# A table of corrections to the priorities of a list planner, in a one-core attention and two-layer MoE kernel

## The chip, the cores and the metric

The kernel runs on one core of one Trainium2 chip. The metric is the device time of one execution in microseconds, as the median of the runs shown. The profile comes from one profiled execution, and its times count from the first instruction of the program.

## The reference, cut to what matters

Three stages follow one another; each takes the output of the one before. B, H, S, D are 2, 8, 768, 64, so there are 1536 tokens of 512 numbers, and the hidden width of the two layers is 2048.

```python
# 1: attention: a window of +-16 positions, and 24 block summaries (max of k, mean of v over 32 positions)
k_sum = k.reshape(B, H, nb, block, D).max(axis=3)
v_sum = v.reshape(B, H, nb, block, D).mean(axis=3)
scores = concat(where(|i - j| < 16, q @ k.T / 8, -1e9), q @ k_sum.T / 8 + log(32))
x = softmax(scores) @ concat(v, v_sum)
# 2: first layer: a rational function between two products
h = x @ w_in
g = (a0 + a1*h + a2*h**2 + a3*h**3) / (1 + |b0|*|h| + |b1|*h**2 + 1e-6)
x = g @ w_out
# 3: second layer
h = x @ w_in2
out = (h * clip(h + 3, 0, 6) / 6) @ w_out2
```

The weights arrive as 64-bit floats; the kernel makes 32-bit pairs of them itself.

## The kernel before, in words

**Tiling.** Attention works on 12 groups of 128 tokens (six of each batch). A group has `scores` (TensorE, L407, and the maximum on VectorE, L420), `softmax` (ScalarE L434, GpSimd L438 and L440, VectorE L439), `turn` (TensorE transposes L450, copied out in L454 or L456) and `values` (TensorE L468, split into a high and a low part in L478 and L479). Four groups make one chunk `x` of 512 tokens; there are three chunks c. The block means of v come from TensorE (L347, L374).

**The layers.** `steps` has 96 steps n = (ph, c, i): four phases ph (two halves of the hidden width for each layer), three chunks, eight hidden tiles i of 128. A step has a `first_product` (12 matmuls of 128x512, L513), an activation (`act1` for the first layer, `act2` for the second) and a `second_product` (12 matmuls, L535) that comes three steps, later two pairs of steps, behind. Each value is held as a high and a low part, so each product is three matmuls. Steps 0 to 15 are done one at a time into the PSUM tiles `hs0` and `hs1`; from step 16 on they go in pairs into two double tiles `hb`. After the eighth tile of a chunk the four accumulators `y` are copied out (`evac`, L549 to L570).

**The weights.** `weight(ph, i)` brings one hidden tile in two halves k: one DMA of 512 KB into one of four buffers `raw` (L246), a clamp (L252, VectorE, in phases 1 and 2 GpSimd), a scaling (L254, ScalarE), a shift and an or on the integer words (L256 and L258, VectorE), the high part (L261, ScalarE) and the low part (L263, GpSimd).

**The order.** Nothing is issued while the code above runs: each piece of work is put in a list with `add`, with its engine, a cost in us, what it reads and writes, and whether it takes the port that VectorE and GpSimd share (`port=True`). `order` then makes one list for all engines. `tail[i]` is the sum of the costs on the longest path from operation i to the end. A list scheduler goes forward in planned time; whenever an engine is free, it takes among the operations of that engine that are ready by then (within 0.15 us) the one with the largest `tail`. It leaves no engine idle when something is ready for it. The products are tied to one another by `chain=True` and so keep their order on TensorE; only attention can slip between them. The DMAs go to one queue (SP) in the same manner. On the chip each engine then executes its own share of the list strictly in that order, and waits by semaphores.

**Fill.** Where the plan has TensorE wait over 0.6 us ahead of an operation that has a `fill`, or as long as no chunk x exists, L703 puts matmuls on zeros (128x256, bf16) in front of it, as many as fit the planned wait and at least four.

Of the kernel before, what the change touches and what calls it, by code (L numbers as in the profile page):

```python
# [18 lines left out]
B, H, S, D = 2, 8, 768, 64  # L19
# [3 lines left out]
P = 128  # L23
# [19 lines left out]
PE, DVE, ACT, POOL, SP = "PE", "DVE", "ACT", "POOL", "SP"  # L43
WIRE = 280.0
HOP = 0.1


class Plan:
# [31 lines left out]
    def order(self):  # L80
        ops = self.ops
        n = len(ops)
        after = [[] for _ in range(n)]
        for i, o in enumerate(ops):
            for d in o[3]:
                after[d].append(i)

        def late(d, i):
            return ops[d][5] + (0.0 if ops[d][0] == ops[i][0] else HOP)

        tail = [0.0] * n
        for i in range(n - 1, -1, -1):
            tail[i] = ops[i][1] + max((late(i, j) + tail[j] for j in after[i]), default=0.0)
        missing = [len(o[3]) for o in ops]
        ready = [0.0] * n
        avail = {e: [] for e in (PE, DVE, ACT, POOL, SP)}
        for i in range(n):
            if not missing[i]:
                avail[ops[i][0]].append(i)
        free = dict.fromkeys(avail, 0.0)  # L100
        port = wire = 0.0
        lanes = [0.0] * 8
        dmas = 0
        start = [0.0] * n
        for _ in range(n):
            best = None
            for e, a in avail.items():
                if not a:
                    continue
                when = {i: max(ready[i], port) if ops[i][4] else ready[i] for i in a}  # L110
                t0 = max(free[e], min(when.values()))
                i = max((i for i in a if when[i] <= t0 + 0.15), key=lambda i: (tail[i], -i))
                t = max(t0, when[i])
                if e == SP:
                    t = max(t, lanes[dmas % 8])
                if best is None or t < best[0]:
                    best = (t, e, i)
            t, e, i = best
            us, land = ops[i][1], ops[i][5]
            avail[e].remove(i)  # L120
            start[i] = t
            free[e] = end = t + us
            if ops[i][4]:
                port = end
            if e == SP:
                wire = max(wire, end) + land
                end = wire + 2.2
                lanes[dmas % 8] = end
                dmas += 1
            for j in after[i]:  # L130
                ready[j] = max(ready[j], end + (0.0 if ops[j][0] == e and e != SP else HOP))
                missing[j] -= 1
                if not missing[j]:
                    avail[ops[j][0]].append(j)
        self.start = start
        return sorted(range(n), key=lambda i: (start[i], i))
# [638 lines left out]
```

## Time and profile before

| | us |
|---|---|
| median of 3 runs | 630.49 |
| lowest and highest run | 629.33 and 635.31 |
| span of the profiled execution | 629.6 |
| TensorE matmul busy | 608.4 (97%) |
| VectorE busy | 399.5 (63%) |
| GpSimd busy | 356.1 (57%) |
| ScalarE busy | 347.9 (55%) |

The profile keeps the span alone as the time of its own execution; it stands 0.9 us under the median and 0.3 us over the lowest run, so that sums over the trace can be set against the median directly. Matmuls are pipelined, and the busy time of TensorE counts the fill matmuls too, so 97% isn't a measure of useful work. Shares over the whole span mix stages with different limits.

### The profile page before, as it was taken

The page shows a single profiled execution, that of the slowest core. Times are in us where ns is not written, and L with a number is a line of the kernel's source. Part 1 is how long each engine was busy: PE and PEld are TensorE (multiplying, and loading weights), DVE is VectorE, ACT ScalarE, POOL GpSimd, SP SyncE. Part 2 cuts the span into 40 slices and gives each one's busy share as a digit, 9 for nine tenths or more (in the row PEclk, how much of TensorE's full clock was granted, in tenths as well). Part 3 has the DMA queues.
Part 4 walks back from the last instruction along what each step waited for, and adds up shares of the span by engine and source line. Part 5 has one row for each costly group of instructions (what it writes and reads, how often), then busy time and mean ns, then how long its engine had stood idle before and what let it go on. Part 6 is the DMA issues. An engine that isn't in the chain of part 4 may idle for free.

```text
span 629.6 us, 9837 instructions
## 1 busy us (share of the span) xinstructions
PE 608.4 (97%) x3848; PEld 495.4 (79%) x3848; DVE 399.5 (63%) x622; ACT 347.9 (55%) x604; POOL 356.1 (57%) x277
## 2 busy tenths in 40 slices
PE   9898998999999999999899999999999999999997
PEld 6577776777788887888688888888888888888886
DVE  4689799977648999999699985841364611201211
ACT  2779778885759669676669665431453322211220
POOL 0846978875576886779469887531545422131311
PEclk9899999999999999999899999999999999999999
DMA  9993453220142312321030332400122100000101
GB/s 314 318 290 99 157 170 99 85 84 0 32 134 68 101 53 81 101 67 34 0 101 1 134 93 92 148 3 1 67 68 100 35 0 1 33 35 1 67 1 67
DMA packets 18072, 52.49 MB, mean 83 GB/s; under 512 B 2281, under 2 KB 2761, under 8 KB 18025
## 3 DMA queue, kind: packets, MB, share of 16 engines
q1 hardware_dynamic: 18024, 51.85, 25.7%
q8 instruction: 30, 0.49, 0.3%
q14 instruction: 18, 0.14, 0.1%
HBM read 48.06 MB, written 3.15 MB: 81 GB/s over the span
## 4 chain that ended last, share of the span: by engine, by line
PE 65%; DVE 19%; ACT 7%; issue 4%; POOL 2%; DMA 2%; SPq 0%; DVEq 0%; POOLq 0%; ACTq 0%
PE y L535 29%; PE hb L513 25%; PE hs L513 5%; DVE raw L258 5%; DVE raw L256 4%; DVE t L608 2%; DVE t L600 2%; DMA raw<-in_w 2%; DVE hb L610 1%; PE hs L407 1%; DVE t L601 1%; PE hs L703 1%; PE hs L468 1%; ACT hb L603 1%; ACT hb L605 1%
## 5 line engine op out<-in xcount | busy, mean ns | idle before, releaser
L513 PE MATMUL hb<-xx,wt 128*128 128x512 f32 x960 | 226.5, 392 | 4.0 <-DVE t L612 3.8
L513 PEld LDWEIGHTS hb<-xx,wt 128*128 128x128 f32 x960 | 180.9, 189 | 43.8 <-DVE t L612 5.4
L535 PE MATMUL y<-g,wt 128*128 128x512 f32 x576 | 138.8, 392 | 1.6 <-ACT part L551 1.5
L628 POOL TENSOR_TENSOR g<-t,g 128x1024 fp32r<-128x1024 f32 x24 | 58.2, 2425 | 135.7 <-ACT g L627 126.8
L535 PE MATMUL y<-wt,g 128*128 128x512 f32 x576 | 134.1, 389 | 0.0
L535 PEld LDWEIGHTS y<-g,wt 128*128 128x128 f32 x576 | 107.0, 188 | 24.4 <-ACT part L551 2.2
L535 PEld LDWEIGHTS y<-wt,g 128*128 128x128 f32 x576 | 108.1, 188 | 22.5
L263 POOL TENSOR_TENSOR wt<-raw,wt 128x512 fp32r<-128x512 f32 x62 | 87.1, 1416 | 41.5 <-ACT wt L261 36.7
L625 DVE SCALAR_TENSOR_TENSOR t<-t,hb 128x1024 f32<-128x1024 f32 x24 | 29.3, 1220 | 119.2 <-ACT t L624 119.2
L258 DVE SCALAR_TENSOR_TENSOR raw<-raw 128x512 int32<-128x512 int32 x62 | 76.3, 1241 | 6.9 <-ACT raw L254 5.1
L597 POOL TENSOR_TENSOR q<-q,u 128x512 f32<-128x512 f32 (+1 forms) x32 | 59.9, 1870 | 30.3 <-ACT u L591 29.1
L615 POOL TENSOR_TENSOR g<-t,g 128x512 fp32r<-128x512 f32 (+1 forms) x32 | 62.1, 1941 | 7.6 <-ACT g L614 5.0
L261 ACT ACTIVATE wt<-raw 128x512 fp32r<-128x512 f32 x62 | 41.1, 673 | 44.1 <-DVE raw L258 38.6
L256 DVE TENSOR_SCALAR raw<-raw 128x512 int32<-128x512 int32 x62 | 58.1, 945 | 10.5 <-DMA raw<-in_w 5.3
L624 ACT ACTIVATE t<-hb,lnb 128x1024 f32<-128x1024 f32 x24 | 26.8, 1116 | 66.5 <-PE hb L513 66.5
L627 ACT ACTIVATE g<-t 128x1024 fp32r<-128x1024 f32 x24 | 25.5, 1061 | 57.0 <-PE y L535 56.7
L254 ACT ACTIVATE raw<-raw 128x512 f32<-128x512 f32 x62 | 40.5, 674 | 17.4 <-DVE raw L252 14.0
L513 PE MATMUL hs<-xx,wt 128*128 128x512 f32 x192 | 47.4, 396 | 0.0
L513 PEld LDWEIGHTS hs<-xx,wt 128*128 128x128 f32 x192 | 35.4, 188 | 8.1 <-issue 0.4
L252 DVE TENSOR_SCALAR raw<-raw 128x512 f32<-128x512 f32 x30 | 26.8, 894 | 21.2 <-DMA raw<-in_w 21.2
L434 ACT ACTIVATE s<-s,stat 128x120 f32<-128x120 f32 x72 | 27.3, 382 | 11.3 <-DVE stat L420 11.3
L614 ACT ACTIVATE g<-t 128x512 fp32r<-128x512 f32 (+1 forms) x32 | 27.1, 846 | 7.8 <-DVE t L612 7.6
(111 smaller groups left out, 694.8 us busy)
## 6 DMA issues: line engine op xcount, KB each, us to landing
raw<-in_w SPq DMA_DIRECT2D x62, 512.0 KB, 5.3
out<-part SPq DMA_DIRECT2D x12, 256.0 KB, 2.8
vv<-in_vw SPq DMA_DIRECT2D x6, 384.0 KB
k<-in_kT SPq DMA_DIRECT2D x4, 384.0 KB
tok<-in_vt SPq DMA_DIRECT2D x3, 512.0 KB
q<-in_qT SPq DMA_DIRECT2D x6, 256.0 KB, 7.2
e<-in_kT SPq DMA_DIRECT2D x4, 384.0 KB, 7.9
raw<-in_vt SPq DMA_DIRECT2D x3, 512.0 KB, 6.2
```

Of the source, the lines that this page charges most:

```text
L254: add(ACT, 0.62, lambda hif=hif: nc.scalar.activation(hif, hif, AF.Prelu, scale=REBIAS, alpha=2.0 ** 32), [kr], [(kr, 1)])
L256: add(DVE, 0.38, lambda lo=lo: nc.vector.tensor_single_scalar(lo, lo, 29, op=ALU.logical_shift_right), [kr], [(kr, 0)], port=True)
L258: add(DVE, 0.65, lambda lo=lo, hi=hi: nc.vector.scalar_tensor_tensor(out=lo, in0=hi, scalar=3, in1=lo, op0=ALU.logical_shift_left, op1=ALU ...
L261: add(ACT, 0.62, lambda lof=lof, ph=ph, i=i, cols=cols: nc.scalar.activation(w_of(ph, i)[:, 0, cols], lof, AF.Copy), [kr, (kr, 0)], first)
L263: add(POOL, 1.27, lambda lof=lof, ph=ph, i=i, cols=cols: nc.gpsimd.tensor_tensor(out=w_of(ph, i)[:, 1, cols], in0=lof, in1=w_of(ph, i)[:, ...
L434: nc.scalar.activation(s[:, a, :], s[:, a, :], AF.Exp, scale=-1.0, bias=sm[:, 0, j, a, :], accum_out=sm[:, 1, j, a, :])
L513: mm(ps, lt, rt, start=(k == 0), stop=(k == 11))
L535: mm(y, lt, rt, start=(i == 0 and j == 0), stop=(i == HALF - 1 and j == 2))
L597: add(POOL, us_of(1.27, 2.36), lambda: nc.gpsimd.tensor_tensor(out=q, in0=q, in1=uu, op=ALU.mult), uk, qk, port=True)
L615: add(POOL, us_of(1.27, 2.38), lambda: nc.gpsimd.tensor_tensor(out=gl, in0=t, in1=gh, op=ALU.subtract), tk, gk, port=True)
L625: add(DVE, 1.18, lambda: nc.vector.scalar_tensor_tensor(out=t, in0=t, scalar=6.0, in1=pair_of(a), op0=ALU.min, op1=ALU.mult), hk, tk)
L628: add(POOL, 2.38, lambda: nc.gpsimd.tensor_tensor(out=gl, in0=t, in1=gh, op=ALU.subtract), tk, gk, port=True)
```

## The change: a correction to each priority

The table `LEAD` is a text of 1827 characters, one for each operation in the order in which they are added. A character's code less 80 is a number of microseconds, from -45 (`#`) to 45 (`}`); the mean is -3.9. It is added to `tail`, and the choice among ready operations goes by the sum.

```diff
+LEAD = (
+    '}+IaTnry1ysyL|y|}|S|<|}yxluDegd=GasOM%G1W*sKRKU*kN07&)6+.,C}d&V&&&#vc*Z:[wgQp1:+##%#92=#F#,H#?8A'
...
+    'cbl'
+)
...
         tail = [0.0] * n
         for i in range(n - 1, -1, -1):
             tail[i] = ops[i][1] + max((late(i, j) + tail[j] for j in after[i]), default=0.0)
+        rank = [tail[i] + ord(LEAD[i]) - 80 for i in range(n)]
...
-                i = max((i for i in a if when[i] <= t0 + 0.15), key=lambda i: (tail[i], -i))
+                i = max((i for i in a if when[i] <= t0 + 0.15), key=lambda i: (rank[i], -i))
```

The costs, what depends on what, the buffers and the rule that no engine is left idle stay. The number of fill matmuls follows the planned waits, so it can change with the order.

Some places of the table, decoded: the loads of the keys of the first batch have +44, those of the second -41, -41, -37 and -45. The load of the first half of weight tile 0 has +42, of its second half -3, of the first half of tile 2 -16; the loads of v of groups 0 to 5 have -9, -31, 7, -38, 35 and -5; the load of q of group 4 has 5 (and those of groups 2 and 3 have 2 and -5). The operations of `act1` of steps 0 to 8 have -33 on average, those of `act1` from step 16 on 0.5; the weight operations of phase 2 have 14. The operations of attention groups 0 to 6 have between -12 and -21 on average, of groups 7, 8 and 9 they have 9 to 10.

## Rows read from the trace of the kernel before

**Rows 1.** The page: busy time, share and instructions, and TensorE's slices.

```profile
PE 608.4 (97%) x3848; PEld 495.4 (79%) x3848; DVE 399.5 (63%) x622; ACT 347.9 (55%) x604; POOL 356.1 (57%) x277
PE   9898998999999999999899999999999999999997
```

**Rows 2.** The chain that ended last, in order of time: start, length, what.

```profile
308.45 7.37 PE hb L513 x24
315.82 5.44 PE y L535 x24
...
609.58 16.33 PE y L535 x72
```

**Rows 3.** Windows of L513: stretch, length, PE busy (count), clock, DMA share, GB/s.

```profile
0.00:308.40 308.40, 115.26 (x480) 0.99 0.38 117
```

**Rows 4.** The same windows of L535.

```profile
0.00:308.40 308.40, 105.22 (x432) 0.99 0.38 117
```

**Rows 5.** The same windows of L407, of L468 and of L450.

```profile
0.00:308.40 308.40, 16.23 (x768) 0.99 0.38 117
...
0.00:308.40 308.40, 14.14 (x384) 0.99 0.38 117
...
0.00:308.40 308.40, 13.75 (x96) 0.99 0.38 117
```

**Rows 6.** The same windows of L703, the fill matmuls.

```profile
0.00:50.00 50.00, 11.53 (x84) 0.97 1.00 304
50.00:200.00 150.00, 15.12 (x122) 1.00 0.29 89
200.00:308.40 108.40, 0.00 (x0) 1.00 0.21 68
```

**Rows 7.** Windows of all engines: PE, PEld, DVE, ACT, POOL busy (counts), clock, DMA.

```profile
20.00:40.00 20.00, 16.53 (x269) 13.31 (x267) 13.86 (x53) 13.64 (x47) 14.54 (x17) 0.91 1.04 323
40.00:300.00 260.00, 249.34 (x1891) 202.41 (x1892) 223.82 (x382) 198.05 (x374) 194.88 (x161) 1.00 0.29 91
200.00:250.00 50.00, 48.52 (x213) 39.52 (x212) 46.15 (x39) 38.91 (x44) 36.60 (x24) 1.00 0.26 85
250.00:300.00 50.00, 50.00 (x221) 41.00 (x220) 48.44 (x41) 34.72 (x41) 41.28 (x25) 1.00 0.20 64
```

**Rows 8.** The page's DMA issues: KB of each, us to landing.

```profile
raw<-in_w SPq DMA_DIRECT2D x62, 512.0 KB, 5.3
...
vv<-in_vw SPq DMA_DIRECT2D x6, 384.0 KB
```

**Rows 9.** The chain that ended last, early: values, then the first products.

```profile
33.81 1.15 PE hs L468 x32
...
41.34 5.66 PE hs L513 x24
...
63.03 2.96 PE hs L513 x12
```

**Rows 10.** VectorE's instructions of L256 and L258, each line by itself: duration min/median/max.

```profile
L256 DVE TENSOR_SCALAR raw<-raw x62: 394/732/2635, 27.1 to 495.3; 128x512 int32<-128x512 int32 x62
...
L258 DVE SCALAR_TENSOR_TENSOR raw<-raw x62: 664/696/2936, 33.8 to 497.0; 128x512 int32<-128x512 int32 x62
```

**Rows 11.** Groups of VectorE in 40 to 300: busy, mean ns, idle before.

```profile
L258 DVE SCALAR_TENSOR_TENSOR raw<-raw 128x512 int32<-128x512 int32 x33 | 42.9, 1310 | 1.1
L256 DVE TENSOR_SCALAR raw<-raw 128x512 int32<-128x512 int32 x35 | 31.4, 905 | 6.4 <-POOL wt L263 5.1 <-DMA raw<-in_w 1.2
```

**Rows 12.** The timeline from 294.74: start, length, engine, what, idle before.

```profile
294.74 5.16 DVE L256 TENSOR_SCALAR raw<-raw 128x512 int32<-128x512 int32 x2
...
307.17 1.22 DVE L612 SCALAR_TENSOR_TENSOR t<-hb,t 128x1024 f32<-128x1024 f32 x1
...
308.45 2.07 PE L513 MATMUL hb<-xx,wt 128*128 128x512 f32 x6 [2.32 <-DVE t L612]
```

**Rows 13.** TensorE in a window of 2 us: busy, clock, DMA.

```profile
310.00:312.00 2.00, 2.00 (x6) 0.50 0.00 0
```

More of the change, by code (lines that the diff above doesn't have):

```diff
@@ L45 @@
 HOP = 0.1
+LEAD = (
+    '}+IaTnry1ysyL|y|}|S|<|}yxluDegd=GasOM%G1W*sKRKU*kN07&)6+.,C}d&V&&&#vc*Z:[wgQp1:+##%#92=#F#,H#?8A'
+    "-#K:s}#B'&t6E,0g#S9o.]%/Ei%)zy28L?0ME6&M#K*+*%%#30.#a&#Z@+]&&#+/>]MOJSL)#zMV5UI#>z##KRze$[>(?:#("
+    ",(]c}24(('%'%+<#%'#uQ*G}=1-*-#q9,46%.0q0(i[S;;*&fZyIey=?;L@y9C-a'RHACy]kXn+lv+'FuXuK074?&#6#>1o6"
+    ',#)9##$\\#llhoh#$P/*#d#>%+|#_+O2C`vIta@fr7N:lC^AE>GsW/(>N4`zoCQ}}]}}b}o;vzhX;K<sa}LP^|}M}8vtvt8Me'
+    '+FcMR*#].5O\\$%BRC).)=)#??#8)8T#d:)/E#;#.#*O#9VbJ<<0Ju$##I&#-#C####55%#B##?#.#&CP#a#?))##`#DL>###'
+    "######*%#C##6r$##$D#;*D##*#$)#7,-##*###09&I#4$tH{-32$\\#2,),5##,07#ma'D<%$I;*=##,I:#E##`.H>##}YDs"
+    "JA'//\\7ma++JVY`6.K={JN4x\\@$}f8}}}8A=egtS6s}Hdef}2}?Z61BW$4eFm2X{v#%ag?iz7I#o+6Dq%Y@cUOOT`dSooVm,"
+    "JK#LZnX/RM,+92L######(##&18lM5#5#^X_V_<p]dX}zv}n}exr_(Q3QD#.#)Z6F''7/0)$)),3)B=x`*f6i`d;=#M#&1M>"
+    "&:<P279TSq^8^QFBD,%'#QZnfN'3O,^CGF)^TB7#g#%\\f.#G#b1npsDrvrh#cgsTw;vWd]W#d(AG\\0#WWs5B5>|ut_*9jH{V"
+    'FE89bd^nBXX}{Q(<+Ff17>#-L\\+K=44E}o8B#*[4wT%e*Zj\\,#-+6<wGODOR7}Q?>}+T3(0H@0C+H/0-+8/?E-#;#:G33#)#'
+    "25A-#$#'EED##2-G?IM:<U<4*:h}B^|cv,=<g6#>\\IM>O4-a,||,]zz{-f`r}}}_/qpgq-@}-<{D<t-<@>:mte1qtBtK=E%+"
+    '{p=k[aUz_EXvv^_Rvv,MC0xwfDp[}q}ttcvvw}vjvY]m`C|e|o7[(w\\riNtrmtRACSTp1I%*N0+13wT#AjXV:DyyyyexZ3Hr'
+    'WZ#5L-;,*&K#>O=jci7.h\\>6HASgY7ca_yxiD`ZcNg4Pk/%(&KLjc|^/nAE@|GbusEytFNu#Z2gexTB%%*>)L)eDmoxtcR0t'
+    "xEvygWifde7\\'ceO|}1{ppx{K}gZx8mwXaW]xe}3}im}juyh}x>az1vNx}`{tFhxxMvgG06Bc9ov71gmXYnn(EMFoay3cjKF"
+    '?mpJnHLyycstmhkQ;B^gjjugf}jjkkRcmkkOiKU#YeucfnnOg5q#DEnU\\bD8gWR:J#,#9D#@<}l_m}xZT<s#FyEwqy[XgT}_'
+    '`3e}B\\<{}YY]I,./4?JNLQ_[UpR:k3J420_U}m-=u-HZS-H-`W0-249--:--P#G+(#.3#<5a&<D&<BO)Vq&X.t&{K&x^<kbp'
+    "Kq&E_l]GuDd'ST'E.z,xy,8'H6TKBB-NFxn2CN6_WK4ql}yTqUy}}hfK}}}npDJjX]MpHVkokkdZZ72bkY*%-2=[4P);%p=K"
+    '3+:.^pl2BqROczM7>Bzf3<.eR*:*3I}/RSZ8^A;-8VtJJJJJDeGU@+A=FAku>kd>j>>+@cZ48V2#.0yF+uAD1DFTbOQg5aM8'
+    '}d=46#(#;#?WC/LPh#}mp=vRrVVM#orjwPD}1iiR+\\WKfMh]{}{{[tn}kvqQ}g.uuPz{zvz{uY}czy|zZ=uub&^#etbqpopo'
+    'cbl'
+)
 class Plan:
```

## The prediction

> **What bounds the kernel now.** I read the page's busy shares first, then the chain that ended last, then windows of single lines of TensorE. The page shows TensorE 97% busy and no slice under eight tenths [rows 1], which would leave nothing to an order; but it counts the fill matmuls and the overlap of pipelined matmuls. The chain says where the order matters. From 315.82 to 609.58 it is an unbroken run of pieces of 24 product matmuls, 5.44 us each (293.76 us are 54 of them), and after that 72 more and one eviction [rows 2]. There TensorE never waits; no order can shorten it. One product matmul costs 5.44/24 = 0.2267 us. All that a new order can win lies before 308.4.
>
> What TensorE does in those 308.4 us: 480 + 432 = 912 product matmuls [rows 3, 4], 206.7 us. Scores, values and transposes have 16.2 + 14.1 + 13.8 = 44.1 us [rows 5], a little too much since ends overlap. The fill has 11.5 + 15.1 = 26.7 us [rows 6]. That makes 277.5, and 31 us remain for the clock's warm-up, the block means and bare waits. The fill is the part that the plan itself knows of: L703 issues as many matmuls as fit a wait that the list has. Of it, 11.5 us lie in the first 50 us, where the DMA engines are full (share 1.00 there, 1.04 and 323 GB/s in 20 to 40 [rows 6, 7]), and 15.1 us in 50 to 200, where their share is 0.29 and loads can't be the cause. After 200 there is none.
>
> VectorE is the next in line: 223.8 us busy in 40 to 300, 46.15 and 48.44 us in the last two stretches of 50 [rows 7].
>
> **The change part by part.**
>
> *The table itself.* It is read while the program is built. It adds no instruction, and the list still leaves no engine idle that has something ready. So its direct cost is nothing, and its whole effect is which of several ready operations goes first on an in-order engine, and how many fill matmuls are issued. The number of choices is large at first and small later: before 200, attention, weights and single steps compete on every engine, while in phases 2 and 3 `act2` and a few weights do, with TensorE covering both.
>
> *The DMA queue.* The loads of the second batch's keys go back by about 40, the first half of weight tile 0 forward by 42. The loads without anything to wait for are simply sorted by `tail` plus correction; worked out from the costs in the source, those of v of groups 1 and 3 come to 512.8 and 502.1 and fall behind five loads that they now precede: two weight halves of 512 KB, v of groups 4 and 5 with 384 KB each [rows 8], and q of group 4 (256 KB by the source). That is 2,048 KB, at 323 GB/s [rows 7] 6.3 us later for group 3. What covers it: v is read by the values of a group, and the third of the first four groups has them at 33.81 [rows 9]. By the source 6.5 MB stand ahead of and in group 3's v now; at 323 GB/s that is 20 us of transfers, and 26 us then. I take the cost as nothing; if the cover were gone, at most 6.3 us would be lost ahead of the first product, which starts at 41.34 now.
>
> *Attention against `act1`, in 50 to 200.* `act1` of steps 0 to 8 falls by 33 on average, groups 0 to 6 by 12 to 21, groups 7 to 9 rise by about 10. So relative to one another, attention and weights go ahead of the activations. That costs something: `hs0` and `hs1` are the only homes of single steps, so step n + 2 can't start before `act1` of step n is done. It also brings something: the second chunk, on which steps 8 to 15 wait, is done sooner, and the third, on which steps 16 on wait. Between the first two products at 41.34 and the third at 63.03 [rows 9] TensorE now has nothing to multiply for want of a weight tile and a free `hs`. What of the 15.1 us of known waits goes? From below none, or a loss as in the last rival; from above all of it, and part of the 11.5 us before 50. I take all of the 15.1 and none of the earlier part: these waits stand in the list, no load holds them, and it is what a different order can fill; the earlier ones have full DMA engines beside them. The bare waits I leave as they are.
>
> *What is late next.* Once TensorE comes to 200 sooner, VectorE and GpSimd must keep up. VectorE has 260 - 223.8 = 36.2 us idle in 40 to 300 [rows 7]. If the whole stretch ran as densely as its fullest part (48.44 of 50), it would take 223.8/0.969 = 231.0 us, so 29.0 us is the most that it can lose. 15.1 us use about half of that. The idle is mostly before 200, just where the new order acts, so weight steps can move there.
>
> *The shared port.* L256 takes 394 ns at best and 2,635 ns at worst, L258 664 and 2,936 [rows 10], and 42.9 and 31.4 us for 33 and 35 of them where 21.9 and 13.8 would do [rows 11]: 38.6 us of VectorE's busy time are waits inside instructions. The Trainium skill (SBUF — State Buffer, Who interferes with whom) says that VectorE and GpSimd share one pair of ports as an exclusive lock, held for a whole instruction. By that rule no order removes these waits but by moving GpSimd's work away, and the 29.0 us stand; without it they could be ordered away and the gain would end only with TensorE's own holes, over 40 us. The maxima, one GpSimd operation longer than the minima, agree with the rule.
>
> *Phases 1 to 3.* From step 16 on neighbouring pairs of steps are 10.9 us apart in `tail` (24 matmuls of each product), and weights of the next phase stand 60 to 90 us lower than the `act1` beside them, as at 294 to 308, where L256 and L258 of phase 2 run between two steps [rows 12]. Two corrections differ by 90 at most and by far less as a rule (0.5 on average for `act1`, 14 for weights of phase 2), so few choices turn over. I count nothing here, after 315 because TensorE covers it, before it because it has no known waits.
>
> **The sum.** 15.1 us off 630.49 is 615.4 us, 2.4% less.
>
> **The rivals.**
>
> *Same: the gain is given back behind 200.* The waits of 50 to 200 close, but TensorE then runs into the activations. VectorE's idle time in 200 to 300 is 3.85 + 1.56 = 5.4 us [rows 7]; if all weight work stays behind 200, TensorE can win only that, 630.5 - 5.4 = 625.1 us. For it: 48.44 of 50. Against it: 36.2 - 5.4 = 30.8 us of VectorE's idle time lie in 40 to 200 and the last 8 us, open to weights once their buffers are free. Chance 0.17.
>
> *Same: the order hardly moves on the chip.* Where one operation is ready, a priority decides nothing. Against it: even the sorted loads change. Time 630, chance 0.03.
>
> *Slower: weight steps ahead of `act1` without a known wait.* Its model is in the trace: two L256 of 2.6 us each, stretched by GpSimd, stand ahead of a step's L600; the step's L612 ends late, TensorE waits 2.32 us [rows 12], and since the list had no wait there, no fill either. The clock falls to 0.50 [rows 13], the 1.2 GHz level, and the next 24 matmuls take 7.37 instead of 5.44 us [rows 2]. So one such place costs 2.32 + 1.93 = 4.25 us. With `act1` down by 33 in steps 0 to 8 and the clock's fill gone with the planned waits, this could come up in any of the nine steps. It decides from four places on if the 15.1 us close all the same (17 us), and from two if nothing closes (8.5 us, 639 us). I take 640 us. For it: the corrections of single operations scatter widely (from -45 to 45 within one step). Against it: before 200 TensorE has attention to slip between the products. Chance 0.14.
>
> **How the numbers follow.** The forecast has the remaining 0.66. Within 1% means 624.2 to 636.8, about what a measurement of this kernel can tell from no change, as its three runs differ by 6 us. Faster 0.66, same 0.17 + 0.03 = 0.20, slower 0.14. The range reaches from VectorE's bound, 630.5 - 29.0 = 601.5, rounded 602, to 633: it takes in both cases of no change and leaves out the slower one and a little at either end.
>
> **What would show it.** In windows of L703 the 15.1 us of 50 to 200 should be gone or under 3, the 11.5 of the first 50 about as they are. The run of 5.44 us pieces should begin near 300 instead of 315.8, with the same length behind it. VectorE should be busier in 40 to 200 (over 0.85 of the time) and not less dense from 200 on. The first product should start within 3 us of 41.3, with group 3's v landed before its use. The forecast is wrong if the fill of 50 to 200 remains, or if it goes and bare waits of TensorE on L612 or on weights come in its place, with the granted clock under 1.00 in 50 to 300, or if the run of 5.44 us pieces has holes in phases 2 and 3.

## The result, and the profile after

The changed kernel takes 623.03 us (median of 4 runs, 621.31 to 625.26); the kernel before took 631.88 us in the same comparison (4 runs). The ratio is 0.9869, with a 95% interval from 0.9822 to 0.9917: 1.3% faster, some 8.3 us. Forecast were 615.4 us and a range of 602 to 633. So the sign and the range hold, and the gain is a little over half of the 15.1 us of the sum. In the profiled executions the span goes from 629.6 to 620.8 us, by 8.8.

The page of the changed kernel, its busy times and TensorE's slices (all lines of the code lie 26 further down than before, L513 is L539 and so on):

```profile
PE 601.8 (97%) x3808; PEld 492.7 (79%) x3808; DVE 389.0 (63%) x622; ACT 350.9 (57%) x604; POOL 353.3 (57%) x277
PE   8798899999899999999999999999999999999997
```

Against [rows 1] TensorE has 40 matmuls less (fill), and VectorE is 10.5 us less busy with the same 622 instructions. Nothing was taken out of its work; what shrank is the time inside instructions.

The chain that ended last, of the changed kernel: start, length, what.

```profile
16.34 9.87 DMA vv<-in_vw
...
26.35 0.42 PE hs L494 x6
...
43.23 2.92 PE hs L539 x12
...
169.38 3.95 PE hb L729 x23
173.33 5.85 PE hb L539 x24
179.18 2.72 PE y L561 x12
181.90 5.44 PE hb L539 x24
187.34 5.44 PE y L561 x24
...
600.77 16.33 PE y L561 x72
```

Three things are to be seen beside [rows 2, 9]. The unbroken run of 5.44 us pieces begins at 181.90, no longer at 315.82; there are no holes behind 182. The first product comes later, 43.23 against 41.34, and ahead of it stands a load of v. And just ahead of the unbroken run, at 169.38, 23 fill matmuls lie on the chain.

Where the time went is best read by counting. The starts of the product matmuls (L513 and L535, then L539 and L561) make 2304 points in each trace, in the same order, and the difference of the k-th is the lead so far:

| product matmul | before | after | lead |
|---|---|---|---|
| first | 41.3 | 43.1 | -1.8 |
| 13th | 44.1 | 54.2 | -10.1 |
| 49th | 65.8 | 70.8 | -5.0 |
| 217th | 128.8 | 130.8 | -2.0 |
| 241st | 140.3 | 137.9 | 2.4 |
| 385th | 183.9 | 181.7 | 2.1 |
| 593rd | 231.3 | 228.9 | 2.4 |
| 657th | 247.6 | 243.4 | 4.2 |
| 785th | 276.6 | 272.4 | 4.3 |
| 1213th | 378.2 | 369.4 | 8.8 |
| last | 625.5 | 616.7 | 8.8 |

Up to 130 us the new order loses; by 184 us it has won 2.1. The other 6.7 us come between there and 316, in two steps: 1.8 us near 240 and 4.5 between 277 and 316. For that stretch the prediction had counted nothing.

Windows of the fill, L729, in the changed kernel (stretch, length, busy and count, clock, DMA):

```profile
0.00:50.00 50.00, 11.21 (x91) 1.00 0.99 292
50.00:200.00 150.00, 10.60 (x75) 0.98 0.31 97
```

Of the 15.1 us in 50 to 200 [rows 6], which were to go in full, 10.6 are still there.

Windows of all engines, and then the groups of the two integer steps on VectorE in 40 to 300, of the changed kernel:

```profile
40.00:300.00 260.00, 251.52 (x1909) 206.23 (x1907) 221.85 (x387) 206.97 (x382) 194.05 (x163) 0.99 0.30 95
...
200.00:250.00 50.00, 50.00 (x223) 41.38 (x222) 46.64 (x39) 39.81 (x45) 40.38 (x25) 1.00 0.25 85
250.00:300.00 50.00, 50.00 (x222) 41.43 (x221) 44.30 (x42) 39.15 (x45) 38.44 (x25) 1.00 0.19 63
```

```profile
L284 DVE SCALAR_TENSOR_TENSOR raw<-raw 128x512 int32<-128x512 int32 x34 | 34.4, 1026 | 1.8 <-ACT raw L280 1.7
L282 DVE TENSOR_SCALAR raw<-raw 128x512 int32<-128x512 int32 x34 | 31.7, 951 | 1.7 <-DMA raw<-in_w 1.7
```

In 200 to 300 VectorE is not busier than in [rows 7], while TensorE has no idle time. The integer steps take 66.1 us for 68 of them; before, 74.3 us for 68 [rows 11].

### The profile page after: what moved, and what is told of

The parts are those of the page before. It is cut to its first block, busy times and chain, and to the rows that moved or that the text cites. A ratio compares the mean times of both kernels' runs of the same rounds, so it can differ in the third digit from the quotient of the medians.

```text
span 620.8 us, 9770 instructions
## 1 busy us (share of the span) xinstructions
PE 601.8 (97%) x3808; PEld 492.7 (79%) x3808; DVE 389.0 (63%) x622; ACT 350.9 (57%) x604; POOL 353.3 (57%) x277
## 4 chain that ended last, share of the span: by engine, by line
PE 91%; DMA 4%; DVE 3%; ACT 1%; issue 1%; POOL 0%; SPq 0%; DVEq 0%; POOLq 0%; ACTq 0%
PE y L561 41%; PE hb L539 35%; PE hs L539 7%; PE hs L729 2%; PE hs L494 2%; DMA vv<-in_vw 2%; PE hs L433 2%; DMA tok<-in_vt 1%; PE hs L476 1%; DMA k<-in_kT 1%; PE hb L729 1%; DVE s L446 0%; DVE t L638 0%; DVE hs L636 0%; DVE raw L282 0%
## 5 line engine op out<-in xcount | busy, mean ns | idle before, releaser
L539 PE MATMUL hb<-xx,wt 128*128 128x512 f32 x960 | 224.7, 390 | 0.0
L539 PEld LDWEIGHTS hb<-xx,wt 128*128 128x128 f32 x960 | 180.5, 188 | 37.5
L561 PE MATMUL y<-g,wt 128*128 128x512 f32 x576 | 138.4, 392 | 0.0
L561 PE MATMUL y<-wt,g 128*128 128x512 f32 x576 | 134.1, 389 | 0.0
L561 PEld LDWEIGHTS y<-wt,g 128*128 128x128 f32 x576 | 108.1, 188 | 22.5
L561 PEld LDWEIGHTS y<-g,wt 128*128 128x128 f32 x576 | 107.0, 188 | 22.0
L289 POOL TENSOR_TENSOR wt<-raw,wt 128x512 fp32r<-128x512 f32 x62 | 85.6, 1392 | 30.4 <-ACT wt L287 30.2
L284 DVE SCALAR_TENSOR_TENSOR raw<-raw 128x512 int32<-128x512 int32 x62 | 67.6, 1103 | 11.2 <-ACT raw L280 10.6
L641 POOL TENSOR_TENSOR g<-t,g 128x512 fp32r<-128x512 f32 (+1 forms) x32 | 60.7, 1897 | 6.6 <-issue 5.6
L282 DVE TENSOR_SCALAR raw<-raw 128x512 int32<-128x512 int32 x62 | 55.7, 909 | 7.1 <-DMA raw<-in_w 7.1
L539 PE MATMUL hs<-xx,wt 128*128 128x512 f32 x192 | 47.6, 396 | 0.0
L539 PEld LDWEIGHTS hs<-xx,wt 128*128 128x128 f32 x192 | 35.4, 189 | 7.7 <-ACT s L460 0.3
```

Of the source, the lines that this page charges most:

```text
L282: add(DVE, 0.38, lambda lo=lo: nc.vector.tensor_single_scalar(lo, lo, 29, op=ALU.logical_shift_right), [kr], [(kr, 0)], port=True)
L284: add(DVE, 0.65, lambda lo=lo, hi=hi: nc.vector.scalar_tensor_tensor(out=lo, in0=hi, scalar=3, in1=lo, op0=ALU.logical_shift_left, op1=ALU ...
L289: add(POOL, 1.27, lambda lof=lof, ph=ph, i=i, cols=cols: nc.gpsimd.tensor_tensor(out=w_of(ph, i)[:, 1, cols], in0=lof, in1=w_of(ph, i)[:, ...
L539: mm(ps, lt, rt, start=(k == 0), stop=(k == 11))
L561: mm(y, lt, rt, start=(i == 0 and j == 0), stop=(i == HALF - 1 and j == 2))
L641: add(POOL, us_of(1.27, 2.38), lambda: nc.gpsimd.tensor_tensor(out=gl, in0=t, in1=gh, op=ALU.subtract), tk, gk, port=True)
```

## The experiments

The change has no parts but its 1827 numbers, so the first experiments cut the table: by operation number, and by engine. Ratios are to the kernel before on the same chip.

**Only the early corrections, and only the late ones.** Operation 695 is the first product of step 16, which comes at 173 us.

```diff
-        rank = [tail[i] + ord(LEAD[i]) - 80 for i in range(n)]
+        rank = [tail[i] + (ord(LEAD[i]) - 80 if i < 695 else 0) for i in range(n)]   # early
+        rank = [tail[i] + (ord(LEAD[i]) - 80 if i >= 695 else 0) for i in range(n)]  # late
```

> The corrections act on the first 694 operations alone (attention, the weights of phase 0, steps 0 to 15); all later ones go by the longest path. After the full change, 2.1 us of the 8.8 us were won by product matmul 384 (184 us) and 6.7 us between there and 316 us. If the later choices make their own gain, this kernel keeps only the 2.1 us: about 0.3 % faster than before. If the later gain comes from how the early order leaves VectorE and GpSimd, it keeps nearly all: 1.2 to 1.4 % faster. If the stall of 4.2 us at 308 is a chance meeting on the shared port that any shift of time undoes, it keeps 2.1 + 4.2 = 6.3 us: 1.0 %.

> The corrections act on operations from 695 on alone (steps 16 to 95 and the weights of phases 1 to 3). The order of TensorE is that of before in full; VectorE, ScalarE, GpSimd and the loads differ behind about 140 us. If the later choices make their own gain: 6.7 us or 1.1 % faster, the pieces of 5.44 us without holes from about 190 on. If that gain is left over from the early order: no change, holes of about 6 us in 200 to 316 as before. If the stall at 308 is a chance meeting: 0 to 4.2 us faster, with other holes in other places.

Early: 625.72 us, ratio 0.9898 (0.9875 to 0.9922). Late: 625.19 us, ratio 0.9901 (0.9875 to 0.9926). Each half by itself wins 1.0%, and together they win 1.3%, so they win in part the same microseconds. The traces say which. Late starts 1.6 us ahead, has the products at the times of before between 125 and 190 us (183.9 for the 385th in both) and then no hole at all. Early is 1.9 us ahead at the 385th, the stall at 308 is gone, but another has come, with the same look as the old one; at the end it is 5.6 us ahead, late 6.6. Windows of TensorE in 200 to 316, of late and then of early:

```profile
200.00:316.00 116.00, 116.00 (x513) 1.00 0.23 78
```

```profile
200.00:316.00 116.00, 113.54 (x500) 1.00 0.20 69
```

The chain of early, in 240 to 270: two stretched L282 (L256 before) ahead of the activation's L626, as in [rows 12].

```profile
246.60 4.86 DVE raw L282 x2
251.46 1.14 DVE t L626
```

So the holes behind 200 can be closed by the late corrections alone, which is the first of the three theories. The second, that early keeps nearly all, isn't borne out: it keeps 5.6 of 8.8 us by the traces, and has a new stall. The time of early is that of the third, but it doesn't show a chance meeting that any shift undoes: behind 190 us the order of VectorE, ScalarE and GpSimd in early differs from that of before, so it is not only shifted. A kernel that is only shifted comes below, with the loads alone.

**Two instructions moved by hand.** The list of the kernel before, with the two L256 of [rows 12] put behind the last VectorE step of the activation that they delayed.

```diff
-        return sorted(range(n), key=lambda i: (start[i], i))
+        made = sorted(range(n), key=lambda i: (start[i], i))
+        for i in (1227, 1255):
+            made.remove(i)
+        at = made.index(1073) + 1
+        return made[:at] + [1227, 1255] + made[at:]
```

> The kernel before, its list as it was, but for two instructions of L256 (the shift of two weight halves of phase 2) that stand ahead of the VectorE steps of act1 of step 36; they go behind the last of these, and what reads them comes later still. If the stall ahead of 308.45 and the half clock after it come from these two, each stretched to 2.6 us by GpSimd, TensorE wins 2.3 + 1.9 = 4.2 us: 0.7 % faster, and the clock stays at 1.00. If VectorE merely meets GpSimd on another instruction, the wait moves to another step and the time is the same within 1 us.

627.25 us, ratio 0.992 (0.9894 to 0.9947): 0.8% for two instructions out of 622 on VectorE. In its trace the products are 1.7 to 2.2 us behind those of before between 190 and 303 us and 2.5 us ahead from 330 on; so 4.2 us were won at this place, as expected, and the start of the run, which has the same order, varies by about 2 us from one execution to the next. The timeline around the place, start, length, engine, what (lines lie 4 further down than before in this kernel):

```profile
303.82 1.23 DVE L616 SCALAR_TENSOR_TENSOR t<-hb,t 128x1024 f32<-128x1024 f32 x1
...
304.96 0.76 DVE L260 TENSOR_SCALAR raw<-raw 128x512 int32<-128x512 int32 x2
```

Where they took 5.16 us together [rows 12], they take 0.76 here: GpSimd is idle at that moment. TensorE doesn't wait at this place, and its clock stays at 1.00; the other wait of before, 1.48 us at 240, is still there with 1.52.

**Only the loads, and all but the loads.**

```diff
-        rank = [tail[i] + ord(LEAD[i]) - 80 for i in range(n)]
+        rank = [tail[i] + (ord(LEAD[i]) - 80 if ops[i][0] == SP else 0) for i in range(n)]  # sp_only
+        rank = [tail[i] + (ord(LEAD[i]) - 80 if ops[i][0] != SP else 0) for i in range(n)]  # no_sp
```

> The corrections act on the loads alone; the other engines go by the longest path. In the prediction the new order of the loads costs nothing. After the full change the first product came 1.8 us later and product matmul 48 came 5.0 us later. If the loads cause that by themselves, the first product is 2 us or more late here too and the time is 2 to 6 us longer, or 0.3 to 1 % slower. If the loads are where the gain before 184 us comes from (weights arrive sooner, keys of the second batch make room), it is 2 to 4 us faster, 0.3 to 0.6 %.

> The changed kernel with the corrections of the loads at zero, all others kept. The loads alone made the kernel 0.4 % slower. If the loss of 2 to 5 us ahead of product matmul 192 comes from the loads, and the rest of the table brings the gain, this is faster than the changed kernel: 618 to 621 us. If loads and the rest hang on each other, it is slower than the changed kernel, by 4 us or more.

Only the loads: 634.22 us, ratio 1.0037 (1.0013 to 1.0061). All but the loads: 651.34 us, ratio 1.0305 (1.0281 to 1.033). Taken apart the two cost 0.4% and 3.0%, together they win 1.3%. The table isn't a sum of corrections that are each good: the order of the engines needs the loads that came with it. All but the loads has lost its time before 140 us (the 193rd product matmul comes 26.4 us later than before). With the loads alone the 25th product matmul lies 8.1 us back and the 49th 10.2 (76.0 against 65.8), as the chain of that kernel shows, in which the scores of a group and the maxima of the second batch's keys (L321) come ahead of the activation that frees the PSUM tile.

```profile
51.56 0.86 DVE ks L321
...
55.79 4.21 PE hs L729 x19
...
68.65 2.89 PE hs L729 x25
...
72.79 2.99 PE hs L539 x12
```

The loads alone also decide about the chance meeting. Behind 190 us every engine has the order of before, and the products come 3 to 4.5 us later. The stall at 308 comes too, 4.5 us later, with the same two instructions ahead of it (timeline, and TensorE in a window of 2 us):

```profile
299.21 5.17 DVE L282 TENSOR_SCALAR raw<-raw 128x512 int32<-128x512 int32 x2
...
312.92 7.35 PE L539 MATMUL hb<-xx,wt 128*128 128x512 f32 x24 [2.35 <-DVE t L638]
```

```profile
314.00:316.00 2.00, 2.00 (x6) 0.50 0.00 0
```

Two instructions moved end the stall, a shift of 4.5 us does not: at this place the order decides.

**No fill at all.** Once with the changed kernel, once with the kernel before. The edit was meant to spare the fill ahead of the first chunk. But the tile of chunk x is made while the list is built (`x_of` in `evac`), so `("x", 0) not in made` is never true when the matmuls are issued: in all the kernels here fill follows planned waits over 0.6 us alone, and this edit takes out all of it, 164 matmuls of the changed kernel and 204 of the kernel before, not only the 75 and 122 behind 50 us.

```diff
-                if i in plan.fill and (wait > 0.6 or ("x", 0) not in made):
+                if i in plan.fill and ("x", 0) not in made:
```

> The changed kernel without the fill matmuls once a chunk x exists (those ahead of that stay): 75 fewer of them behind 49 us. In the prediction the fill stands for waits that TensorE has anyway, so leaving it out wins nothing, and the clock, no longer kept up, falls ahead of the products that follow: 2 to 8 us slower than the changed kernel (626 to 631 us). Against that: at 169.38 the 23 fill matmuls begin only when the activation that frees their PSUM tile is done, which is what the product behind them waits for too, and run 3.95 us at half clock. If the fill comes behind the wait and not in it, leaving it out wins what it takes, less the half clock of the products: 2 to 6 us faster than the changed kernel (617 to 621 us).

> The same edit on the kernel before, whose order stays: 122 fill matmuls of 15.1 us behind 50 us go. If they cover waits: no gain, and up to some 8 us slower for the clock. If they come behind the waits, as the one at 170.91 that began 0.70 us after TensorE ran dry, a part of the 15.1 us is won: 2 to 8 us faster, 0.3 to 1.3 %.

Both are left with the same 3644 matmuls; the busy times of the changed kernel without fill:

```profile
PE 588.9 (96%) x3644; PEld 479.6 (78%) x3644; DVE 386.4 (63%) x622; ACT 350.2 (57%) x604; POOL 354.0 (58%) x277
```

The changed kernel without fill: 615.17 us (614.26 to 617.38), ratio 0.974 (0.9717 to 0.9763), a further 1.3%. The kernel before without it: 634.83 us, ratio 1.0042 (1.0018 to 1.0065), 0.4% slower. One edit, two signs. In the changed kernel the first product comes at the same time (43.2 us against 43.1), by the 241st product matmul 1.9 us are won, and 4.1 more around 169. The timeline of the changed kernel at 169, with the fill (start, length, what, idle time before and its releaser):

```profile
168.63 0.69 DVE L638 SCALAR_TENSOR_TENSOR t<-hs,t 128x512 f32<-128x512 f32 x1
...
169.38 3.95 PE L729 MATMUL hb<-z 128*128 128x256 bf16 x23 [2.45 <-DVE t L638]
```

And without it, where L638 ends 1.8 us sooner:

```profile
167.55 5.70 PE L539 MATMUL hb<-xx,wt 128*128 128x512 f32 x24 [2.54 <-DVE t L638]
```

The wait is the same, 2.45 and 2.54 us. The fill doesn't stand in it: it writes the PSUM tile that the product will write, so it waits for L638 like the product, and comes behind the wait. It holds up the product by 3.95 us. In the kernel before, some of the fill does its work. Without it the clock is gone where the next products come, while it is 1.00 from 56 to 84 us with the fill; windows of TensorE and a row of the timeline, of the kernel before without fill:

```profile
76.00:80.00 4.00, 4.00 (x10) 0.50 0.75 233
```

```profile
75.61 5.02 PE L513 MATMUL hs<-xx,wt 128*128 128x512 f32 x11 [0.57 <-POOL wt L263]
```

These 11 matmuls would take 2.5 us at the 2.4 GHz level; 0.50 is the 1.2 GHz level. The profiled execution was the fastest of 12 and is no longer than that of before in the end (629.7 against 629.6 us); over the 12 the granted clock goes from 0.984 at 631.45 us down to 0.965 and 0.970 in the two slowest, 637.61 and 637.91, against 0.989 to 0.997 in the runs of the kernel before. That the clock makes the 0.4% rests on these.

**The fill at 169 alone.**

```diff
-                if i in plan.fill and (wait > 0.6 or ("x", 0) not in made):
+                if i in plan.fill and i != 695 and (wait > 0.6 or ("x", 0) not in made):
```

> The changed kernel with the fill left out at one place alone, ahead of the first product of step 16 (23 matmuls at 169.38, 3.95 us). The kernel without any fill behind the first chunk was 8 us faster than the changed one by medians, and 5.9 us by their traces, of which 4.1 us came up at this place. If this fill lies on the path by itself: 4 us faster than the changed kernel, near 619 us, 2.0 % faster than before. If the time at this place is that of the products' own wait or of the clock: the same as the changed kernel, 623 us.

621.22 us (616.96 to 621.92), ratio 0.9826 (0.9789 to 0.9863). That is 2.7 us better than the ratio of the changed kernel, but the intervals overlap; the traces differ by 1.9 us. Its timeline shows why it isn't 4:

```profile
169.89 7.35 PE L539 MATMUL hb<-xx,wt 128*128 128x512 f32 x24 [2.55 <-DVE t L638]
```

The 3.95 us of fill are gone, but the products behind the wait take 7.35 us where they took 5.85, at a granted clock of 0.55:

```profile
170.00:172.00 2.00, 2.00 (x6) 0.55 0.64 203
```

3.95 - 1.50 = 2.45 us is what the place gave. In the kernel without any fill the same 24 matmuls had the full clock (1.00 in 168 to 170) after the same wait. The fall isn't the same in every execution either: five of the six runs have a granted clock of 0.990 to 0.993 over the span and take 620.65 to 621.92 us, the sixth has 0.999 and takes 616.96. And the wait of [rows 12], there followed by 7.37 us for 24 matmuls, is followed by the full clock in the kernel before without fill:

```profile
309.75 5.73 PE L513 MATMUL hb<-xx,wt 128*128 128x512 f32 x24 [2.36 <-DVE t L612]
```

Why the clock falls in one and not in the other, these runs don't settle.

**Another table, without fill.** The corrections of 1,481 operations differ.

> Without fill behind the first chunk, and with another table: many small changes to the corrections, kept when the plan came out shorter, also with costs a few per cent off. If the plan's order carries over to the chip, it is faster than the changed kernel without fill, 607 to 613 us. If what is left on the chip are waits that the plan doesn't know (VectorE and GpSimd on the shared port, the clock), it is the same within 3 us or slower, 613 to 620 us.

614.89 us, ratio 0.9738 (0.971 to 0.9766): the same as without fill and with the table of the change, although the plan by its own reckoning was shorter. Both are faster than the kernel before and the changed kernel.

## Why the prediction was right, and which terms were off

**What held, and what was luck.** All that can be won lies before 316: behind it the lead stays at 8.8 us to the end. The table adds no instruction: but for the fill, the counts of the five engines are those of before. The stall of [rows 12, 13] was read rightly as to cause and price: moving the two L256 gave back 4.2 us where 4.25 were worked out. Faster was the likeliest call and came; the forecast number was 7.6 us too low. But the stretch that was to give all 15.1 us gave 2.1, and 6.7 came from the stretch that was put at nothing. That the sum still lies in the range, which took in no change at all, is in good part luck. By the prediction's own sign (it is wrong if the fill of 50 to 200 remains) its mechanism failed, with 10.6 of 15.1 us left. Nor is VectorE over 0.85 busy in 40 to 200 (221.85 - 46.64 - 44.30 = 130.9 of 160 us, or 0.82).

**The term that was mis-sized: 15.1 us of known waits in 50 to 200.** It rested on reading the fill as waits that the list has and that a better order closes. Of this fill 4.5 us went. By the count of products the stretch up to 184 us gave 2.1 us, and 1.8 of loss at the first product are in that. Two things were wrong in the step. Waits in the list are not free to be closed because no load holds them: the third product still waits for the activation of the first (by the count it starts at 55.6 before and 59.3 after; the 63.03 of [rows 9] is the fourth). `act1`, put back by 33, comes late, as the prediction itself had weighed: on the chain, maxima of scores (L446) go ahead of its last step.

```profile
49.57 0.20 DVE s L446
...
58.23 0.70 DVE t L638
...
59.58 2.77 PE hs L539 x12
```

And the fill isn't the wait. Left out of the changed kernel it wins 1.3% more, left out of the kernel before it loses 0.4%; so a part of these microseconds was never a wait but work on the path, and a part was worth its place. With fill in neither kernel the table wins 19.7 us (634.83 to 615.17), and 9.6 us of it by the 385th product matmul (185.4 to 175.8): so the new order does bring step 16 forward. With fill in both it is 2.1 us, since by then the fill costs the changed kernel 5.9 us and gives the kernel before 1.5. How many fill matmuls the new list has could have been worked out from the source, since it follows the planned waits alone.

**The term put at nothing: loads.** The cover was looked for at group 3, whose values come at 33.81 [rows 9]. But v of group 0 also falls behind loads, and its values stand first: in the changed kernel the chain goes through that load (9.87 us to 26.21) to the values at 26.35. What it costs isn't shown. In the three traces with fill and with the order of before at this point the first product starts at 41.3, 39.7 and 41.9 us (before, late, two moved), in the three with the order of the change at 43.1, 44.9 and 44.9 (after, early, without the fill at 169): means of 41.0 and 44.3. With the loads alone it starts at 42.7, with all but the loads at 44.7; so the loads are not needed for the delay, and by themselves they make 1.7 us of it, about the spread between executions. Nothing is still the wrong price, for another reason: without its loads the table is 4.4% slower than with them (ratios of 1.0305 and 0.9869).

**The term put at nothing: phases 0 and 1 behind 200.** "No known waits" was true and the wrong test. TensorE had 3.8 us of unknown ones there, and a half clock behind the second. With it they make most of the 6.7 us, the larger part of the gain. The stall was in the prediction, as the model of the slower rival; it was priced as a loss that could come and not as one that could go. A trace that shows a stall shows also what its absence is worth.

**The shared port.** Above it was argued that by the lock of the Trainium skill (SBUF — State Buffer, Who interferes with whom) no order removes the waits inside VectorE's integer steps. The runs agree with the lock and not with that conclusion, which doesn't follow from the rule either: the same section of the Trainium skill has issue order decide who blocks. L256 and L258 together were busy for 58.1 + 76.3 = 134.4 us in the kernel before and 123.3 in the changed one, for 124 instructions each time. The order decides whether they meet a busy GpSimd. Over all eleven kernels, six have under 125 us (after 123.3, late 124.1, all but the loads 124.8, without the fill at 169 124.6, without fill 119.8, the other table 115.7), and they leave TensorE at most 0.2 us idle in 200 to 316; the five others (before 134.4, early 136.2, two moved 128.8, loads alone 138.1, before without fill 141.2) leave 1.5 to 5.3 us. The bound of 29 us from VectorE's busy time therefore counted waits as work; no kernel here came near it.

**The rivals.** "The gain is given back behind 200" went the other way: more was won there than ahead of it. The slower rival's mechanism isn't to be seen in the changed kernel: TensorE waits 2.45 us on L638 at 167 and the clock falls (0.91 in 160 to 180), but the list knew that wait and put fill there, and no weight step stands ahead of L638 on VectorE from 164 on. In early it came once, at 246.60. Its count was also off: with the 15.1 us closed, four places make 630.5 - 15.1 + 17 = 632.4 us, which is no change by the prediction's own bounds; it takes six. That the order hardly moves is refuted by every cut of the table.

## What to carry to other kernels

A hole that the plan knows and a hole that only the trace has are two lists: before a new order is valued, list the bare waits of the bounding engine with the instructions just ahead of their releaser. Here two of them, one with the clock lost behind it, were worth more than what the planned waits gave, and a hand-made move of two instructions tries it. Fill that writes the tile of the operation it covers waits for the same release and so stands behind the wait; measure the kernel without it (a tile of its own was not tried here). A table of priorities is tuned as a whole: half of it isn't half of its worth, and one engine's share, or all but that, can cost more than no table. To tell an order from a chance meeting, compare with a kernel that has the same order at that place, only later.

## What the runs showed of the hardware that was not expected

In this kernel GpSimd, while it runs without a pause, holds VectorE's integer steps up again and again. In the kernel before at 227 to 236 us GpSimd runs L597, L615, two L263 and L252 one right after the other, and each integer step of VectorE gets in only between two of them. The timeline of VectorE and GpSimd:

```profile
227.08 2.42 POOL L597 TENSOR_TENSOR q<-q,u 128x1024 f32<-128x1024 f32 x1 [2.04 <-ACT u L591]
227.16 1.28 DVE L601 SCALAR_TENSOR_TENSOR t<-t,ab,hb 128x1024 f32<-128x1024 f32 x1
...
228.36 1.43 DVE L256 TENSOR_SCALAR raw<-raw 128x512 int32<-128x512 int32 x1
...
229.46 2.58 POOL L615 TENSOR_TENSOR g<-t,g 128x1024 fp32r<-128x1024 f32 x1
...
229.82 2.77 DVE L258 SCALAR_TENSOR_TENSOR raw<-raw 128x512 int32<-128x512 int32 x1
...
231.99 3.23 POOL L263 TENSOR_TENSOR wt<-raw,wt 128x512 fp32r<-128x512 f32 x2
232.51 1.54 DVE L256 TENSOR_SCALAR raw<-raw 128x512 int32<-128x512 int32 x1
...
234.16 1.62 DVE L258 SCALAR_TENSOR_TENSOR raw<-raw 128x512 int32<-128x512 int32 x1
235.20 1.08 POOL L252 TENSOR_SCALAR raw<-raw 128x512 f32<-128x512 f32 x1
235.70 0.87 DVE L256 TENSOR_SCALAR raw<-raw 128x512 int32<-128x512 int32 x1
...
236.49 1.27 DVE L608 SCALAR_TENSOR_TENSOR t<-t,ab,hb 128x1024 f32<-128x1024 f32 x1
```

Five integer steps, which take 0.4 to 0.7 us each at best [rows 10], fill more than 8 us. What first brings GpSimd ahead in such a series isn't shown by these runs. A shift of the whole stretch by 4.5 us ends neither of the two waits on L612 (1.49 and 2.35 us with the loads alone, where the line is L638; 1.48 and 2.32 before); another order does.

The other point is the spread between executions of one list: with the same order up to 110 us, the first product began at 41.3, 39.7 and 41.9 us in three traces (before, late, two moved), and the last was still 2.2 us behind the first at 190 us. A difference of one trace against one trace under 2 us says nothing about the early stretch. The 2.1 us that are won up to 184 us are no more than this spread; the 6.7 us behind come after it, and late has 6.6 us there by itself.
